# Splitting the first weight's conversion into two parts of four groups, in a fused attention and two-layer-pair kernel whose order is planned

## The chip, the cores and the metric

The kernel runs on one core of one Trainium2 chip. The metric is the device time of one execution in microseconds (us), lower is better. The kernel before took 978.41 us (median of 3 runs, 978.08 to 980.85).

## The reference

Masked attention over 4 batches, 8 heads, 576 positions and a head size of 64, in float32; its output (2304 tokens of 512) goes through two feed-forward blocks one after the other, each with weights of 512 x 2048 and 2048 x 512. The weights arrive as float64.

```python
scores = np.matmul(q, k.transpose(0, 1, 3, 2)) / np.sqrt(64)
thresh = np.max(scores, axis=-1, keepdims=True) - tau
scores = np.where(scores >= thresh, scores, -1000000000.0)
attn = np.exp(scores - np.max(scores, axis=-1, keepdims=True))
attn = attn / (np.sum(attn, axis=-1, keepdims=True) + 1e-09)
x = np.matmul(attn, v)                      # then (2304, 512)
h = x @ w_in                                # first block: moe_
sp = np.where(h > 20.0, h, np.log1p(np.exp(np.minimum(h, 20.0))))
x = (h * np.tanh(sp)) @ w_out
h = x @ w_in                                # second block: moe2_, other weights
return (h * np.clip(h + 3.0, 0.0, 6.0) / 6.0) @ w_out
```

## The kernel before

**Attention.** The 32 (batch, head) slices are worked on as 16 pairs of heads, four pairs a batch. An attention tile is 128 queries of one head against all 576 keys. TensorE writes its scores into one of two score buffers (line 1847), VectorE takes the negated peak (`nm_pk`, line 1856), ScalarE the threshold (1861) and the exponential (1866), VectorE masks (`e_ex`, line 1869), ScalarE writes the high float16 part of the result (1874), GpSimd its low part (a subtraction, line 730, `p_ph`), a transposing DMA on SP's queue turns both (`pt_tr`, 1882), and TensorE multiplies with V (1895). V too is split in a high part (ScalarE, line 1792) and a low part (VectorE, line 1797, `vl`). After two tiles of each head of a pair, VectorE normalises (1965 to 1972), TensorE transposes (`aux_fl`, 2009), and ScalarE and VectorE write the result's high and low float16 part into the block's input `x` (`x_fl`, lines 2018 and 730). A batch has 36 tiles: the first 16 complete block 2b (256 tokens), the other 20 block 2b + 1 and the tail of 64 positions. So block 0's input is ready some time after the 16th tile, block 1's after the 36th. A ninth block holds the four tails.

**The feed-forward layers.** Each weight has 8 groups. A group of the first two weights is 1 MB of float64 words, which arrive by one DMA (`raw_lr`, two buffers) and are turned into two float16 parts: VectorE takes the maximum (`top`, line 786), a small matmul spreads it over the partitions, VectorE makes the scales (798 to 803), ScalarE expands the high words (920), GpSimd multiplies (two instructions, line 927), VectorE joins the low words (line 940), ScalarE writes the high part (959), GpSimd the low part (two instructions, line 730, `w__h`). In this trace the groups of `w_in` have the buffer names `cvt_c__1_` 373, 443, 683, 826, 956, 1260, 1378 and 1599, their weight tiles `w__h__1_` 532, 616, 793, 972, 1172, 1375, 1510 and 1734, in this order.

The first layer (`inner` and `gemm1`, line 1239) works on a block group by group: 24 matmuls of 256 columns into one buffer `h`, taken by ScalarE or VectorE with a scale (1288, 1290) and stored to DRAM. Blocks 0 to 5 are worked on between attention's matmuls (`PIECE` = 2 matmuls at a time), blocks 6 to 8 after them. All its matmuls are one chain (`chain["g1"]`): they are issued in the order in which `inner` is called, block after block. The rest follows after attention: Mish and the first block's output matmul (`first_layer`, line 1354, `y_y`, with the second weight), then the second block (`second_layer`, lines 1428 and 1581).

**What sets the order.** When the program is built, a planner (`Plan`) replays all tasks with a cost for each engine and a due time, and appends them to the engines' queues in the order that it finds. On the chip each engine works its queue in order and waits by semaphores; the planned times themselves have no effect there. A task becomes a candidate when what it depends on is planned; each engine takes, of the candidates that can start first (within a small window), the one with the smallest due time. Due times are counted in steps: attention tile t is due at `START + t * STEP`, its product with V `PV_OFF` steps later, its block's input `PV_OFF + FLIP` steps later. Group g of the first weight is due at `START + CONV_AT * STEP + 2 * g * STEP`, hence at 27.1 us for the first and 66.2 for the last; the second weight's from `START + OUT_AT * STEP` = 430 us on. V's loads are due from `START - V_FIRST * STEP` on. Block 0's first-layer work is due from `START + (16 + MOE_LAG) * STEP` on, block 1's from 36 steps in place of 16. `NUDGE` moves the due times of single tasks by name; it has 1596 entries. `WHO` says which engines may take which task: K's scaling (`kh`) is ScalarE's (line 1767), V's low part VectorE's. Some tasks are `idle`: they issue no instruction and only take planned time on VectorE. `input_scales` writes the factors with which the first layer's results are taken, for batch 0 in four parts of two groups, for the other batches once all groups are there.

Of the kernel before, what the change touches and what calls it, by code (L numbers as in the profile page):

```python
# [10 lines left out]
F16 = mybir.dt.float16  # L11
# [36 lines left out]
STEP = 2.791  # L48
START = 12
PV_OFF = 3.422  # L50
V_FIRST = -0.435
FIRST_AHEAD = 3
PREP_AHEAD = 5.76
CONV_STEP = 1
CONV_AT = 5.423
LATE_STEP = 3.76
OUT_STEP = 2.681
OUT_AT = 149.789
V_AHEAD = 4.749
MOE_OFF = 9.75  # L60
MOE_LAG = 13.595
RATE = 0.9
NX = 3
FLIP = 3.348
ALPHA = {"act": 7.907, "pe": 3.022}
FITS = 0.015
# [3 lines left out]
BACKLOG = 99.0  # L70
# [16 lines left out]
SLOW = 0.413  # L87
SLOW_LATE = 0.226
HASTE = -5.307
WHO = {  # L90
    "c20": ("dve",), "c21": ("pool",), "c30": ("pool", "dve"), "c31": ("pool", "dve"),
    "q2": ("pool",), "q3": ("pool", "dve"), "u20": ("dve",), "u21": ("pool",),
    "u30": ("pool",), "u31": ("pool", "dve"), "uy0": ("pool", "dve"), "uy1": ("dve",),
    "kh": ("act",), "vh": ("act",), "vl": ("dve",), "q": ("dve",), "o0": ("dve",), "o1": ("dve",),
# [3 lines left out]
JOIN = 2.448  # L98
JOIN_FROM = 340.468
STAY = 0.954  # L100
# [333 lines left out]
PAD = {"zp": 0.834, "zpy": 0.374, "zps": 1.772}  # L434
NEAR_LATE = {"pe": 0, "dve": 0.087, "act": 0, "pool": 0.606, "sp": 0.21}
OFF_LATE = 6.941
OFF_FINAL = 29.238
LATE_AT = 11.587
OFF_SECOND = 40

# [1784 lines left out]
```

## Time and profile before

| | |
|---|---|
| time, median of 3 runs | 978.41 us (978.08 to 980.85) |
| profiled execution | 978.92 us |
| its span | 977.1 us, 25813 instructions |
| TensorE matmuls | 919.2 us busy (94%) |
| VectorE | 769.6 us (79%) |
| ScalarE | 650.0 us (67%) |
| GpSimd | 402.3 us (41%) |

The span runs from the first to the last thing that the profiler recorded; the time of the profiled execution is 1.8 us longer. In what follows PE is TensorE's matmuls and PEld its weight loads, DVE is VectorE, ACT ScalarE, POOL GpSimd, SP the engine that issues the DMAs (SPq its queue), and L940 is line 940 of the kernel. A busy share over the whole span is a mean over stages with different limits, so the rows further below are cut by stage. Instructions of one engine can overlap by a little; busy time counts an instant once. The granted clock (PEclk) is that of TensorE as a share of its upper level, 2.4 GHz; its other level is 1.2 GHz.

### The profile page before, as it was taken

How to read it: one execution, taken by the hardware profiler on the slowest of the kernel's cores; microseconds unless marked ns; L12 is line 12 of the kernel's file. 1: busy time of each engine (PE TensorE's matmuls, PEld its weight loads, DVE VectorE, ACT ScalarE, POOL GpSimd, SP SyncE). 2: the span in 40 equal slices, each digit the busy share in tenths (PEclk: the TensorE clock that was granted, in tenths of full speed). 3: DMA queues.
4: the chain of work that ended last, by engine and by line, in shares of the span. 5: the costliest groups of instructions: out<-in, count | busy, mean ns of one | idle time of the engine just before them, and what ended most of it. 6: DMA issues, size and time to landing. Idle time of an engine off the chain costs nothing.

```text
span 977.1 us, 25813 instructions
## 1 busy us (share of the span) xinstructions
PE 919.2 (94%) x10776; PEld 794.8 (81%) x10776; DVE 769.6 (79%) x1444; ACT 650.0 (67%) x1051; POOL 402.3 (41%) x354
## 2 busy tenths in 40 slices
PE   3669689999999999999999999999999999999996
PEld 1447457777777778888888888999999999999986
DVE  7988698888888887469999889787767767758864
ACT  6778688888888877568866778565354444444541
POOL 2777576756655767225656777710000000000000
PEclk9879799999999999999999999999999999999999
DMA  9899999999999999864665756760110110110001
GB/s 319 192 237 226 235 232 232 242 252 224 231 231 273 205 221 237 254 247 165 232 217 187 274 188 265 250 224 2 60 61 2 60 58 6 60 41 22 23 17 29
DMA packets 201796, 164.46 MB, mean 168 GB/s; under 512 B 174160, under 2 KB 174928, under 8 KB 195280
## 3 DMA queue, kind: packets, MB, share of 16 engines
q1 hardware_dynamic: 201680, 162.82, 61.6%
q8 instruction: 85, 1.39, 0.6%
q14 instruction: 31, 0.25, 0.1%
HBM read 84.28 MB, written 36.04 MB: 123 GB/s over the span
## 4 chain that ended last, share of the span: by engine, by line
PE 77%; DVE 11%; DMA 3%; POOL 3%; ACT 2%; issue 2%; SPq 1%; DVEq 0%; ACTq 0%; POOLq 0%
PE h_g L1239 15%; PE y_y L1354 13%; PE s_s L1847 8%; PE aux_pv L1895 6%; PE h_g0a L1428 5%; PE hp_g1a L1428 5%; PE hp_g1d L1428 2%; PE h_g0d L1428 2%; DMA raw_lr<-in_moe_w_in 2%; DVE top L786 1%; DVE e_ex L1869 1%; PE h_g1b L1428 1%; PE hp_g0b L1428 1%; POOL p_ph L730 1%; DVE gs_h L1334 1%
## 5 line engine op out<-in xcount | busy, mean ns | idle before, releaser
L730 POOL TENSOR_TENSOR p_ph<-e_ex,p_ph 128x128 f16<-128x128 f32 (+3 forms) x160 | 186.3, 1187 | 108.7 <-issue 54.8
L1581 PEld LDWEIGHTS <-gs_h 128*128 128x128 f16 x1512 | 146.6, 98 | 18.3 <-issue 1.5
L1428 PEld LDWEIGHTS <-w__h 128*128 128x128 f16 x2016 | 155.8, 98 | 0.6
L1856 DVE TENSOR_REDUCE nm_pk<-s_s 128x1 f32<-128x576 f32 x144 | 104.6, 750 | 29.6 <-PE s_s L1847 28.5
L1869 DVE SCALAR_TENSOR_TENSOR e_ex<-s_s,thr_th,e_ex 128x576 f32<-128x576 f32 x144 | 111.7, 810 | 18.4 <-ACT thr_th L1861 13.6
L1866 ACT ACTIVATE e_ex<-s_s,nm_pk 128x576 f32<-128x576 f32 x144 | 104.2, 730 | 17.9 <-DVE nm_pk L1856 14.0
L1847 PE MATMUL s_s<-kd_lk,qs_qp 64*128 64x288 f32 x440 | 81.3, 485 | 36.4 <-DVE e_ex L1869 27.6
L1874 ACT ACTIVATE p_ph<-e_ex 128x576 f16<-128x576 f32 x144 | 95.2, 679 | 13.0 <-DVE e_ex L1869 9.9
L1428 PEld LDWEIGHTS <-w__u 128*128 128x128 f16 x1008 | 98.5, 98 | 0.0
L1895 PEld LDWEIGHTS <-pt_tr 128*128 128x128 f16 x2016 | 79.9, 102 | 10.9 <-issue 6.1
L1847 PEld LDWEIGHTS s_s<-kd_lk,qs_qp 64*128 64x128 f32 x440 | 42.1, 207 | 57.3 <-issue 40.3
L730 DVE TENSOR_TENSOR gs_h<-g_ab,gs_h 128x896 f16<-128x896 f32 x72 | 74.5, 1085 | 15.9 <-ACT gs_h L1531 15.9
L1895 PE MATMUL aux_pv<-vh,pt_tr 128*128 128x65 f16 (+1 forms) x1296 | 84.7, 202 | 1.5 <-DMA pt_tr<-p_ph 1.3
L1531 ACT ACTIVATE gs_h<-g_ab 128x1792 f16<-128x1792 f32 x36 | 59.6, 1690 | 27.4 <-DVE g_ab L730 27.4
L1895 PE MATMUL aux_pv<-vl_vl,pt_tr 128*128 128x64 f16 x720 | 69.6, 201 | 0.0
L1515 ACT ACTIVATE g_ab<-g_ab,aux,hscales 128x512 f32<-128x512 f32 x72 | 54.1, 805 | 16.9 <-DVE g_ab L1456 16.9
L1288 ACT ACTIVATE he_t<-h_g,hin 128x512 f32<-128x512 f32 x63 | 42.9, 683 | 21.6 <-PE h_g L1239 17.7
L1325 ACT ACTIVATE hp_e<-hl_l 128x512 f32<-128x512 f32 x72 | 42.4, 595 | 21.5 <-DVE gs_h L1334 21.0
L1521 DVE SCALAR_TENSOR_TENSOR g_ab<-g_ab,f 128x512 f32<-128x512 f32 x72 | 51.1, 745 | 5.0 <-ACT g_ab L1515 5.0
L1334 DVE SCALAR_TENSOR_TENSOR gs_h<-hp_e,fscales,gs_h 128x512 f16<-128x512 f32 x72 | 52.9, 742 | 2.2 <-ACT gs_h L1328 1.9
L1328 ACT ACTIVATE gs_h<-hp_e,fscales 128x512 f16<-128x512 f32 x72 | 47.4, 679 | 9.7 <-PE y_y L1354 9.1
L1446 ACT ACTIVATE s_ka<-h_g0a 128x512 f32<-128x512 f32 x27 | 16.1, 595 | 48.4 <-PE h_g0a L1428 48.2
(653 smaller groups left out, 2522.7 us busy)
## 6 DMA issues: line engine op xcount, KB each, us to landing
hd<-he_t SPq DMA_DIRECT2D x36, 512.0 KB, 4.1
hl_l<-hd SPq DMA_DIRECT2D x18, 1024.0 KB, 5.9
raw_lr<-in_moe_w_in SPq DMA_DIRECT2D x16, 1024.0 KB, 5.8
raw_lr<-in_moe_w_out SPq DMA_DIRECT2D x16, 1024.0 KB, 7.4
yd<-yl_zhy SPq DMA_DIRECT2D x9, 896.0 KB, 3.8
qs_qp<-in_q SPq DMA_DIRECT2D x10, 576.0 KB, 5.7
v_lv<-in_v SPq DMA_DIRECT2D x16, 320.0 KB, 4.7
kd_lk<-in_k SPq DMA_DIRECT2D x15, 288.0 KB, 4.1
```

The source lines that it names most:

```text
L730: engine[e].tensor_tensor(dst, a, b, ALU.subtract)
L1239: mm(hv[:, j, :], wj[:, wl, c * P : (c + 1) * P], x.tile[:, c, xl, :], start=j == 0 and n == 0, stop=j == 1 and n == 11, skip_group_check= ...
L1334: nc.vector.scalar_tensor_tensor(s.tile[:, k, 1], g.tile.rearrange("p (a n) -> p a n", a=2), fs[:, fp : fp + 1], s.tile[:, k, 0], ALU.mult ...
L1354: mm(yv[:, h, :], wt[1][f // 2].tile[:, f % 2, wl, c * P : (c + 1) * P], gs[fp // COL].tile[:, fp % COL, gl, f % 2, :], start=fp == 0 and ...
L1428: mm(dst.tile[:, i * Q : (i + 1) * Q], wt[2][fp][wl].tile[:, right - 1, c * P : (c + 1) * P], x[xl].tile[:, c, left - 1], start=first and ...
L1581: mm(region(p), part[:, gl, left - 1], wt[3][fp][wl].tile[:, right - 1], start=fp == n == 0 and spot(p)[1] == 0, stop=fp == NG - 1 and n == 2,
L1847: mm(s[j].tile[:, half, :HALF], lh[r], rh[r], start=m == 0, stop=m == len(terms) - 1,)
L1856: nc.vector.tensor_reduce(neg.tile[:, j : j + 1], sv(j), AX.XY, ALU.max, negate=True)
L1866: nc.scalar.activation(ev(j), sv(j), AF.Exp, bias=neg.tile[:, j : j + 1])
L1869: nc.vector.scalar_tensor_tensor(ev(j), sv(j), thr.tile[:, j : j + 1], ev(j), ALU.is_ge, ALU.mult)
L1874: nc.scalar.activation(p16.tile[:, js, :S], e_.tile[:, js], AF.Copy)
L1895: mm(ov[:, dst, :d], pt.tile[:, j, ch, :], part.tile[:, src, vc, :], start=i == j == ch == 0 and part is vh, stop=j == w - 1 and ch == 8, ...
```

## The change

The first weight (`w_in` of the first block) is converted in two parts. Groups 0 to 3 (`FIRST` = 4) are due from `START + CONV_AT * STEP` on, which is now 7.0 us, and 5.6 us apart. Groups 4 to 7 are due from `START + SECOND_AT * STEP` = 120.6 us on and 8.4 us apart. The weight's summary is due at step 150. The first layer does block 0 with groups 0 to 3, then block 1 with groups 0 to 3, then block 0 with groups 4 to 7, then block 1 with these. Blocks 0 and 1 have two input buffers of their own (`r_xa`), and the three of `r_x` are left to the later ones. Batch 1's input scales are made in four parts like batch 0's, and for groups 4 to 7 of both batches become due when they are ready.

In the planner the `idle` tasks go, some assumed costs change, and the constants are new: START 12 to 9.178, STEP 2.791 to 2.786, PV_OFF 3.422 to 2.279, FLIP 3.348 to 3.912, V's first loads due at START + 0.841 steps in place of 0.435, BACKLOG 99 to 8 (a DMA other than a transpose is planned only when the planned backlog of DMAs is under 8 us), the second weight due from 455 us on and 8.9 us a group (430 and 15.0 before). K's scaling goes from ScalarE to GpSimd; V's low part stays on VectorE. `NUDGE` shrinks from 1596 entries to 121, of which 115 names were there before, most with other values. In the core of the diff, without `NUDGE` and some constants:

```diff
-PV_OFF = 3.422
-V_FIRST = -0.435
+PV_OFF = 2.279
+V_FIRST = -0.841
-CONV_AT = 5.423
+CONV_AT = -0.767
-BACKLOG = 99.0
+BACKLOG = 8
-    "kh": ("act",), "vh": ("act",), "vl": ("dve",), "q": ("dve",), "o0": ("dve",), "o1": ("dve",),
+    "kh": ("pool",), "vh": ("act",), "vl": ("dve",), "q": ("dve",), "o0": ("dve",), "o1": ("dve",),
+SUM_AT = 150
+FIRST = 4
+SECOND_AT = 40.0
+SECOND_STEP = 1.507
...
             at = prio + 2 * g * off
+            if m == 0 and g >= FIRST:
+                at = START + (SECOND_AT + 2 * (g - FIRST) * SECOND_STEP) * STEP
             task = tasker(at)
...
-        a = task({"dve": 1.28}, idle if m < 2 else c3, b, [raw, t], "c" + nm)
-        a = task({"dve": 1.28}, c4, [a], [raw, t], "c" + nm)
+        if m > 1:
+            b = [task({"dve": 1.28}, c3, b, [raw, t], "c" + nm)]
+        a = task({"dve": 1.28}, c4, b, [raw, t], "c" + nm)
...
-        parts = len(scaled_parts) if i == 0 else 1
+        parts = len(scaled_parts) if i < 2 else 1
...
+            if i < 2 and part * NG // parts >= FIRST:
+                task = tasker(None)
-            after = scaled_parts[part] if i == 0 else [f for fs in scaled_parts for f in fs]
+            after = scaled_parts[part] if i < 2 else [f for fs in scaled_parts for f in fs]
...
-    def inner(blk, early, at=None, gap=0.0):
+    def inner(blk, early, at=None, gap=0.0, fps=range(NG)):
...
-        for fp in range(NG):
+        for unit, fp in enumerate(fps):
...
+    r_xa = ring("xa", ap, 2, [P, NCH, 2, BLK], F16)
...
-                    x_of[blk] = Buf(r_x), []
+                    x_of[blk] = Buf(r_xa if blk < 2 else r_x), []
...
-                inner(blk, True, at, gap)
+                if blk == 0:
+                    inner(0, True, at, gap, range(FIRST))
+                elif blk == 1:
+                    gap *= NG / (2 * NG - FIRST)
+                    inner(1, True, at, gap, range(FIRST))
+                    inner(0, True, at + FIRST * gap, gap, range(FIRST, NG))
+                    inner(1, True, at + NG * gap, gap, range(FIRST, NG))
+                else:
+                    inner(blk, True, at, gap)
```

## Rows read from the trace of the kernel before

**Rows 1.** Busy time by stretch: length, engines' busy us, clock, DMA share, GB/s.

```profile
core 0: us, PE busy (x) PEld busy (x) DVE busy (x) ACT busy (x) POOL busy (x), PEclk, DMA share, GB/s
0.00:72.00 72.00, 39.98 (x368) 26.83 (x369) 60.70 (x116) 51.52 (x88) 43.28 (x52) 0.83 0.91 250
72.00:98.00 26.00, 24.84 (x283) 19.73 (x281) 21.30 (x47) 22.23 (x42) 20.12 (x20) 1.00 0.97 227
98.00:120.00 22.00, 14.18 (x132) 9.16 (x130) 13.54 (x32) 14.28 (x25) 11.67 (x14) 0.77 1.03 227
120.00:140.00 20.00, 15.80 (x178) 11.46 (x178) 17.75 (x40) 17.77 (x34) 16.13 (x14) 0.91 1.04 256
140.00:380.00 240.00, 238.04 (x2882) 185.69 (x2881) 200.24 (x363) 199.74 (x371) 151.46 (x141) 1.00 1.08 235
380.00:420.00 40.00, 39.84 (x456) 35.52 (x455) 23.29 (x55) 23.69 (x44) 14.71 (x14) 1.00 0.84 257
420.00:900.00 480.00, 478.48 (x5671) 443.47 (x5669) 380.80 (x696) 290.71 (x415) 144.92 (x102) 1.00 0.36 129
...
sum 977.00, PE 919.25 PEld 794.79 DVE 769.60 ACT 650.04 POOL 402.29; mean PE 114.91 PEld 99.35 DVE 96.20 ACT 81.25 POOL 50.29
```

**Rows 2.** The masks of attention (line 1869) by stretch: VectorE's busy time, count.

```profile
72.00:120.00 48.00, 10.26 (x13) 0.89 1.00 227
120.00:140.00 20.00, 4.87 (x7) 0.91 1.04 256
140.00:380.00 240.00, 76.50 (x99) 1.00 1.08 235
```

**Rows 3.** Groups, 0 to 140 us: count, busy us, mean ns, idle before.

```profile
L786 DVE TENSOR_REDUCE top<-raw_lr 128x1 f32<-128x1024 f32 x9 | 10.9, 1214 | 6.2 <-DMA raw_lr<-in_moe_w_in 6.1
...
L730 POOL TENSOR_TENSOR w__h__1_1172<-cvt_c__1_956,w__h__1_1172 128x512 f16<-128x512 f32 x2 | 2.3, 1158 | 4.3 <-ACT w__h__1_1172 L959 4.3
...
L765 DVE TENSOR_REDUCE top<-aux_zp 128x1 f32<-128x128 f32 x8 | 2.3, 281 | 0.1
...
L927 POOL TENSOR_TENSOR cvt_c__1_956<-cvt_c__1_956,eight 128x512 int32<-128x512 int32 x2 | 2.1, 1056 | 0.8 <-ACT cvt_c__1_956 L920 0.8
...
L801 DVE TENSOR_SCALAR sc<-sc 128x1 f32<-128x1 f32 x9 | 1.4, 153 | 0.3
...
L920 ACT ACTIVATE cvt_c__1_956<-raw_lr,sc 128x1024 f32<-128x1024 f32 x1 | 1.3, 1255 | 0.0
...
L940 DVE SCALAR_TENSOR_TENSOR cvt_c__1_956<-raw_lr,cvt_c__1_956 128x1024 uint32<-128x1024 uint32 x1 | 1.2, 1215 | 0.0
```

**Rows 4.** Waits of VectorE, 72 to 140 us: total, times, longest.

```profile
DVE nm_pk L1856 <- PE s_s L1847: 8.2, 9, 2.5
DVE top L786 <- DMA raw_lr<-in_moe_w_in: 3.6, 1, 3.6
```

**Rows 5.** The chain of waits near 110 us: start, length, what.

```profile
106.36 5.80 DMA raw_lr<-in_moe_w_in
```

**Rows 6.** First-layer matmuls from 60 to 220 us: count, durations, first and last start.

```profile
L1239 PE MATMUL h_g<-x_fl,w__h__1_532 x72: 271/273/273, 72.4 to 187.3; 128*128 128x256 f16 x72
```

**Rows 7.** First-layer matmuls (line 1239) by stretch: TensorE's busy time, count, weight loads.

```profile
72.00:140.00 68.00, 25.02 (x196) 18.28 (x196) 0.90 1.01 236
140.00:380.00 240.00, 125.57 (x1034) 95.78 (x1033) 1.00 1.08 235
```

**Rows 8.** Conversions (line 940) by stretch: VectorE's busy time, count.

```profile
140.00:260.00 120.00, 4.86 (x4) 1.00 1.06 232
260.00:380.00 120.00, 2.43 (x2) 1.00 1.11 238
```

**Rows 9.** Timeline: a mask, the last part of block 1's input; start, length.

```profile
118.72 0.81 DVE L1869 SCALAR_TENSOR_TENSOR e_ex<-s_s,thr_th,e_ex 128x576 f32<-128x576 f32 x1
...
133.82 0.38 ACT L2018 ACTIVATE x_fl<-aux_fl 128x256 f16<-128x256 f32 x1
```

**Rows 10.** Timeline at 72 us: GpSimd's subtractions and a conversion on VectorE.

```profile
72.39 2.51 POOL L730 TENSOR_TENSOR p_ph<-e_ex,p_ph 128x128 f16<-128x128 f32 x2 [0.58 <-ACT p_ph L1874]
...
73.97 2.01 DVE L940 SCALAR_TENSOR_TENSOR cvt_c__1_826<-raw_lr,cvt_c__1_826 128x1024 uint32<-128x1024 uint32 x1
```

More of the change, by code (lines that the diff above doesn't have):

```diff
@@ L46 @@
 RELEASE = dict.fromkeys(("s", "m", "h", "y", "aux"), 0.27)
-STEP = 2.791
-START = 12
-PV_OFF = 3.422
-V_FIRST = -0.435
+STEP = 2.786
+START = 9.178
+PV_OFF = 2.279
+V_FIRST = -0.841
 FIRST_AHEAD = 3
-PREP_AHEAD = 5.76
+PREP_AHEAD = 5.025
 CONV_STEP = 1
-CONV_AT = 5.423
[L56 to L59, printed above, removed]
+CONV_AT = -0.767
+LATE_STEP = 1.5
+OUT_STEP = 1.601
+OUT_AT = 160
+V_AHEAD = 4.836
 MOE_OFF = 9.75
-MOE_LAG = 13.595
-RATE = 0.9
+MOE_LAG = 13.701
+RATE = 0.918
 NX = 3
-FLIP = 3.348
-ALPHA = {"act": 7.907, "pe": 3.022}
-FITS = 0.015
+FLIP = 3.912
+ALPHA = {"act": 6.878, "pe": 2.26}
+FITS = 0
 PORT = ("vl", "c", "u", "o", "zs", "q", "p")
@@ L86 @@
 SLACK = 0
-SLOW = 0.413
-SLOW_LATE = 0.226
-HASTE = -5.307
+SLOW = 0.187
+SLOW_LATE = 0.293
+HASTE = -3.433
 WHO = {
-    "c20": ("dve",), "c21": ("pool",), "c30": ("pool", "dve"), "c31": ("pool", "dve"),
-    "q2": ("pool",), "q3": ("pool", "dve"), "u20": ("dve",), "u21": ("pool",),
-    "u30": ("pool",), "u31": ("pool", "dve"), "uy0": ("pool", "dve"), "uy1": ("dve",),
-    "kh": ("act",), "vh": ("act",), "vl": ("dve",), "q": ("dve",), "o0": ("dve",), "o1": ("dve",),
+    "c20": ("pool", "dve"), "c21": ("dve",), "c30": ("pool",), "c31": ("pool", "dve"),
+    "q2": ("pool", "dve"), "q3": ("pool",), "u20": ("dve",), "u21": ("pool", "dve"),
+    "u30": ("pool", "dve"), "u31": ("pool",), "uy0": ("pool", "dve"), "uy1": ("dve",),
+    "kh": ("pool",), "vh": ("act",), "vl": ("dve",), "q": ("dve",), "o0": ("dve",), "o1": ("dve",),
 }
@@ L97 @@
 PARTS = 4
-JOIN = 2.448
-JOIN_FROM = 340.468
-STAY = 0.954
+SUM_AT = 150
+FIRST = 4
+SECOND_AT = 40.0
+SECOND_STEP = 1.507
+JOIN = 3.144
+JOIN_FROM = 409.647
+STAY = 0.782
 NBLK_EARLY = 2 * B - 2
@@ L103 @@
 NUDGE = {
[323 rows of a table removed]
[25 rows of a table added]
 }
-EASE = {"mk": -6, "ph": 2.117, "pl": 0.391, "tr": 1.5, "ex": 2.281, "s": -5.48, "th": -2.308}
+EASE = {"mk": -6, "ph": 0.526, "pl": -1.615, "tr": 1.702, "ex": 1.842, "s": -6, "th": -1.651}
 P_LO = ("pool",)
@@ L432 @@
 LATE = {"gs": 2, "hl": 2, "h": 2, "y": 2}
-WINDOW = {"pe": 0.17, "dve": 0.095, "act": 0.232, "pool": 0.789, "sp": 0}
[L434 to L438, printed above, removed]
+WINDOW = {"pe": 0.186, "dve": 0.095, "act": 0.226, "pool": 0.722, "sp": 0}
+PAD = {"zp": 0.827, "zpy": 0.3, "zps": 2.577}
+NEAR_LATE = {"pe": 0.013, "dve": 0.075, "act": 0, "pool": 0.694, "sp": 0.21}
+OFF_LATE = 7.635
+OFF_FINAL = 29.067
+LATE_AT = 9.931
 OFF_SECOND = 40
@@ L806, in group_scale @@
         if m % 2 == 0:
-            a = task({"dve": 0.15}, idle, [a], [], "za" + name)
             a = spread(task, name, lambda: top, [], ring, a)
-        return task({"dve": 0.97 if m == 0 else 0.5}, factor, [a], [], "zf" + name)
+        return task({"dve": 0.8 if m == 0 else 0.38}, factor, [a], [], "zf" + name)
     def summary(task, m, ring, after):
@@ L902, in convert @@
             scaled_parts[:] = [factors[i : i + step] for i in range(0, NG, step)]
-        scaled_by[m] = summary(tasker(prio + 2 * NG * off), m, ring, factors)
-    def idle(e):
-        pass
+        at = START + SUM_AT * STEP if m == 0 else prio + 2 * NG * off
+        scaled_by[m] = summary(tasker(at), m, ring, factors)
     def one_conversion(m, g, raw, deps, task):
@@ L1231, in link, with gemm1 @@
         return chain[name]
-    def gemm1(task, m, fp, piece, x, h, ready):
+    def gemm1(task, m, fp, piece, x, h, ready, unit):
         def mms(j, first, end):
@@ L1249, in gemm1 @@
             last = link(
-                task, "g1", fp, piece, lambda a, b, j=j: mms(j, a, b),
+                task, "g1", unit, piece, lambda a, b, j=j: mms(j, a, b),
                 ready + [converted[m, 2 * fp + j]], [x, h, wt[m][fp]], f"g{fp}{j}_",
@@ L1275, in inner @@
         else:
-            x, ready = x_of.pop(blk)
+            x, ready = x_of[blk]
         hscale, scaled = hin[:, blk // 2], hin_done[blk // 2]
-        for fp in range(NG):
+        for unit, fp in enumerate(fps):
             h = Buf(r_h)
-            last = gemm1(task, 0, fp, PIECE if early else 12, x, h, ready)
+            last = gemm1(task, 0, fp, PIECE if early else 12, x, h, ready, unit)
             if fp % 2 == 0:
@@ L1290, in take @@
                     nc.vector.tensor_scalar(dst, h.tile, f, None, ALU.mult)
-            taken.append(task(TAKE, take, [last, scaled[fp]], [h, he], f"t{fp}", 0.0, fp + VECTOR))
+            taken.append(task(TAKE, take, [last, scaled[fp]], [h, he], f"t{fp}", 0.0, unit + VECTOR))
             if fp % 2:
@@ L1298, in inner @@
                 h_stored[blk, fp // 2] = task(
-                    {"sp": 0.5}, put, taken, [he], f"s{fp}", HD_DMA, fp + VECTOR
+                    {"sp": 0.5}, put, taken, [he], f"s{fp}", HD_DMA, unit + VECTOR
                 )
@@ L1934, in query_tiles @@
                 size = (js.stop - js.start) * S
-                cost = {"dve": 0.17 + size / 960.0, "pool": 0.1 + size / 450.0}
+                cost = {"dve": 0.17 + size / 960.0, "pool": 0.35 + size / 490.0}
                 parts.append(
```

348 rows, old and new, of the table NUDGE are left out of this document.

## The prediction

> **What bounds the kernel now.** I read the whole span first and then its stages, because a share over the whole span hides where time can be won. TensorE is busy for 919 of 977 us [rows 1], so the time is TensorE's work, plus what it idles, plus what it loses at a lowered clock. The stages show where that is: 32.0 us idle up to 72 us, 13.2 from 72 to 140, 2.0 from 140 to 380, 0.2 to 420, 1.5 to 900 [rows 1]. The granted clock is below its upper level in the first 140 us and full from there to 900. So from 140 to 900 us TensorE has no room. A gain can only be made before, by work done earlier, and all of it then reaches the end, as TensorE behind is full.
>
> What holds TensorE back before 140 us is read from VectorE. Every attention tile (128 queries of a head) needs a peak and a mask there. From 72 to 120 us come 13 masks, 3.7 us a tile; from 140 to 380 us 99, 2.42 us a tile [rows 2]. In the slow stretch VectorE also converts the first weight: its eight group maxima, and the first of the second weight, all stand before 140 us [rows 3]. From 72 to 140 us VectorE waits 8.2 us for scores and 3.6 for a raw weight load [rows 4]; the chain of waits shows that load, 5.8 us, as what ended last at 112 us [rows 5]: the maximum waits for it at the head of VectorE's queue, and the masks stand behind.
>
> The other half of the picture is the filler, the first layer's matmuls between attention's. Block 0's begin at 72.4 us [rows 6], and by 140 us all eight groups of 24 and four more are done [rows 7].
>
> **The change, part by part.**
>
> *Groups 4 to 7 move behind.* One group costs VectorE 1.214 + 0.281 + 1.215 and four small ops of 0.15, 3.3 us [rows 3], so four cost 13.2; GpSimd 2 x 1.056 + 2 x 1.158 = 4.4, so 17.7; ScalarE an expansion of 1.255 and a copy of as many elements, some 2.5, so 10; and SP's queue four loads of 1 MB, which no longer stand among the transposes. Nothing is saved, all of it is done later: the new due times begin at 9.178 + 40 x 2.786 = 120.6 us and are 8.4 us apart. There these groups take the place of the second weight's, six of which are converted between 140 and 380 us [rows 8], far ahead of their due times (430 us and later). Those move on into VectorE's room: 39.8 us are free from 140 to 380, 16.7 from 380 to 420 [rows 1]. That hides them; with that cover gone they would cost their 13.2 us.
>
> *Block 0 stops after four groups* until block 1's first four are done, as these matmuls are chained in order. So from 72 us until block 1's input is there TensorE has only 4 x 24 x 125.57/1034 = 11.6 us of filler [rows 7]. Block 1's input came 14.7 us behind the mask that ended at 119.5 us, at 134.2 [rows 9].
>
> *What the attention does with the room.* Without conversions a tile cost VectorE (200.24 - 6 x 3.3)/99 = 1.82 us from 140 to 380 [rows 1, 2, 8], so VectorE alone would allow some 2 us. The rate seen with TensorE full is 2.42. I take a rate between 2.2 and 2.42 from 72 us on. A tile's share of TensorE was (238.04 - 125.57)/99 = 1.14 us [rows 1, 2, 7]. At 2.42 us: 13 masks after 72 us are done at 103.5, block 1's input is there at 118.2; until then 46.2/2.42 = 19.1 tiles x 1.14 + 11.6 = 33.4 us of work; then TensorE is full, 21.8; 55.2 by 140 us. At 2.2, by the same steps, 34.1 + 24.7 = 58.8. Before, the busy 54.8 us less 14.18 x 0.23 + 15.80 x 0.09 = 4.7 for the clock are 50.1 [rows 1]; by unit costs, 20 tiles x 1.14 + 196 x 0.121, they are 46.6 [rows 2, 7]. Between these, 48.4, the gain is 6.8 and 10.4; with all bounds 5.1 to 12.2. I take the middle, 8.6.
>
> *Earlier hand-over.* PV_OFF + FLIP fall from 6.77 steps (18.9 us) to 6.19 (17.2), so a block's input is due 1.6 us sooner. Bounds 0 and 1.6; I take 0.8, since due times only order work.
>
> *The first 72 us.* The first four groups are due from 7.0 us on, ahead of most tiles, not from 27.1. VectorE does the same tiles and groups in it, in another order. Bounds: a gain of one maximum with its small ops, some 2 us, and the loss of one raw load that stands ahead of V's, 5.8 [rows 5]; I take 0.
>
> *K's scaling moves to GpSimd* and leaves ScalarE. No row has it on GpSimd; the nearest are 1.06 and 1.16 us for 128x512 [rows 3], so some 1.2 to 1.3 for 128x576, 16 times in 400 us; GpSimd is busy 151 of the 240 us from 140 to 380 [rows 1]. It can also stop VectorE: an op with two inputs in SBUF that met GpSimd's subtractions took 2.01 us and ended 1.1 us behind them; another took 1.215 [rows 3, 10]. Bounds: 0, and 16 x 0.8 = 13 us of VectorE if each met such an op. These ops (16 of V's low part, 16 conversions) are about a tenth of VectorE's time, so I take 1.3 us of VectorE's room and nothing of TensorE's.
>
> The Trainium skill, SBUF — State Buffer, "SBUF: two separate sides", speaks against this move: VectorE and GpSimd share a port pair as an exclusive lock, and whoever comes second is blocked for the other's whole instruction. By it a meeting costs up to all of GpSimd's 1.3 us, 2 us of VectorE's room in place of 1.3; the 2.01 us agree with it.
>
> *Small parts.* The stand-in tasks that leave the planner issued no instruction. Batch 1's input scales become four ScalarE instructions in place of one, under 1 us, in ScalarE's room [rows 1]. Blocks 0 and 1 get x buffers of their own, so holding block 0 longer blocks no other block.
>
> *A new plan everywhere.* The nudges fall from 1596 to 121 and most due times change. From 140 to 900 us TensorE idles only 3.6 us [rows 1], so this can hardly win there: bounds 0 and three times as much again, 11; I take 2.0, half as much again.
>
> Against the profiled execution of 978.92 us (span 977.1 and 1.8 around it; the runs' median is 0.5 less) the sum is - 8.6 - 0.8 + 2.0 = - 7.4, so **971.5**.
>
> **The rivals.**
>
> *Slower: block 0 runs out of filler.* If attention doesn't speed up, because its rate is set by the loop from scores over peak, exponential and mask back to the score buffers, TensorE has less to do than before. At 3.2 us a tile block 1's input is there at 128.3: 17.6 x 1.14 + 11.6 + 11.7 = 43.4 against 48.4, a loss of 5.0, and with the plan's 2.0 the time is 985.9. It decides at 2.87 us a tile. For it: 3.7 us now, and VectorE waits longer for scores than for loads [rows 2, 4]. Against it: 2.42 us later, with the same score buffers.
>
> *No change: the second half comes late.* From 140 to 260 us the conversions of lowest rank came one in 30 us [rows 8]. The filler is 125.57/240 = 52% of TensorE there [rows 7]; a group now opens two units, 5.8 us, which last 11 us. At 15 us a group TensorE lacks 4 x (15 x 0.52 - 5.8) = 8 us, the whole gain: 979. For it: VectorE is at 83% there [rows 1]. Against it: due times 8.4 us apart, ahead of all tiles behind step 49.
>
> *The new plan loses its density:* with 11 us in place of 2.0 the time is 980.5.
>
> *More than forecast:* if the first 72 us tighten too (32 us idle), or a tile takes 2.0 us, 958 to 966.
>
> **How the numbers follow.** About 0.3%, 2.9 us, is what a measurement of this kernel can tell from no change (its runs lie 2.8 us apart). The forecast, 966 to 975.5: 0.43. More than that: 0.14. A small gain or none, by a late second half or a looser plan: 0.25, of which 0.09 still end below 975.5. Slower, by the filler, 981.3 to 990: 0.18. So faster 0.66, same 0.16, slower 0.18. The range 960 to 983 leaves out about a third of the "more" case and most of the slower one, near 0.2.
>
> **What would show it.** Right: no maxima of groups 4 to 7 before 100 us; some 19 masks from 72 to 118 us; block 1's first matmul before 122 us; TensorE idle under 8 us from 72 to 140 us, its clock at the upper level from 100 us on. Wrong: 13 to 15 masks there; a hole of over 12 us on TensorE ahead of block 1's input; first-layer matmuls that wait for conversions behind 140 us; more than 6 us idle from 140 to 900 us; a first y matmul that waits for the second weight.

## The result, and the profile after

The changed kernel takes 989.18 us (median of 4 runs, 986.93 to 990.63), the kernel before 979.41 beside it (978.08 to 980.85): a ratio of 1.0091 [1.0071, 1.011]. It is slower by 9 us where the forecast was a gain of 7, and outside the range. The profiled span is 988.4 us, 11.3 longer than before.

TensorE first, by the stretches of [rows 1]: length, each engine's busy time, granted clock, DMA share, GB/s.

```profile
0.00:72.00 72.00, 37.74 (x328) 24.75 (x328) 59.34 (x115) 46.93 (x78) 53.79 (x57) 0.98 0.89 233
72.00:98.00 26.00, 20.92 (x242) 15.39 (x240) 16.70 (x30) 15.93 (x33) 13.99 (x14) 0.93 1.01 219
98.00:120.00 22.00, 16.85 (x190) 12.47 (x190) 19.84 (x44) 19.37 (x39) 16.84 (x17) 0.89 1.05 213
120.00:140.00 20.00, 15.98 (x177) 11.59 (x178) 16.02 (x31) 14.31 (x27) 14.77 (x12) 0.86 0.95 221
140.00:380.00 240.00, 232.00 (x2780) 182.51 (x2778) 202.65 (x372) 189.15 (x347) 169.32 (x151) 0.99 1.09 232
380.00:420.00 40.00, 39.34 (x474) 33.61 (x471) 24.73 (x61) 23.45 (x45) 21.49 (x21) 1.00 0.93 215
420.00:900.00 480.00, 479.56 (x5621) 444.13 (x5620) 381.22 (x695) 293.51 (x422) 137.75 (x100) 1.00 0.39 140
```

TensorE's idle time is 34.3 us up to 72 us (32.0 before), 14.2 from 72 to 140 (13.2), 8.0 from 140 to 380 (2.0), 0.7 to 420 (0.2), 0.4 to 900 (1.5). With the end that is 66.6 us against 57.9; the other 2.6 us of the span are busy time, although the mean granted clock rose from 0.979 to 0.988. The room that the forecast wanted to fill, 72 to 140 us, is as empty as it was, and a new hole stands behind it. From 420 us on TensorE idles no more than before.

The masks of attention and the first layer's matmuls by stretch, as in [rows 2] and [rows 7]:

```profile
72.00:120.00 48.00, 12.61 (x17) 0.91 1.03 216
120.00:140.00 20.00, 5.20 (x7) 0.86 0.95 221
140.00:380.00 240.00, 72.64 (x94) 0.99 1.09 232
...
72.00:140.00 68.00, 17.13 (x138) 0.90 1.00 218
140.00:380.00 240.00, 126.21 (x1041) 0.99 1.09 232
```

Attention did run faster from 72 to 120 us, 17 masks in place of 13. It was paid for in filler: 138 first-layer matmuls in place of 196. The end of the n-th mask, counted in VectorE's timelines, shows where the tiles are won and lost (us):

```
mask            16     24     36     50     60     70    100    144
before        50.2   76.7  119.5  156.4  181.2  208.4  278.7  389.1
after         57.2   83.2  115.8  152.9  187.1  214.4  287.0  398.5
```

Seven us are lost by the 16th mask, the last that block 0 needs. Ten are won between the 24th and the 36th, where the kernel before converts its second half. Nine are lost again between the 50th and the 60th, and 3.5 more to the end.

The filler in TensorE's timeline: start, length, tile, count. The first row is the last piece of block 0's fourth group, the second the first piece of block 1.

```profile
103.51 1.05 PE L947 MATMUL h_g<-xa_fl,w__h__1_743 128*128 128x256 f16 x8
128.63 0.61 PE L947 MATMUL h_g<-xa_fl,w__h__1_335 128*128 128x256 f16 x4
```

Between them lie 24 us without a first-layer matmul. The same stretch in the changed kernel and then in the kernel before (columns as above):

```profile
104.60:128.60 24.00, 15.97 (x176) 10.92 (x174) 19.93 (x41) 18.67 (x36) 17.96 (x17) 0.79 1.07 245
```
```profile
104.60:128.60 24.00, 17.77 (x185) 12.58 (x183) 15.97 (x34) 17.48 (x34) 16.76 (x17) 0.86 0.98 233
```

What TensorE waits for from 72 to 140 us, then from 140 to 420 us (total, times, longest):

```profile
PE aux_pv L1604 <- DMA pt_tr<-p_ph: 5.9, 3, 3.5
PE s_s L1556 <- DVE e_ex L1578: 5.4, 5, 2.9
...
PE aux_pv L1604 <- DMA pt_tr<-p_ph: 8.0, 9, 3.0
PE s_s L1556 <- DVE e_ex L1578: 0.3, 1, 0.3
```

The same rows of the kernel before, not shown ahead of the prediction:

```profile
PE s_s L1847 <- DVE e_ex L1869: 7.7, 2, 4.5
PE s_s L1847 <- issue: 2.9, 1, 2.9
PE aux_pv L1895 <- DMA pt_tr<-p_ph: 0.9, 2, 0.7
...
PE aux_pv L1895 <- DMA pt_tr<-p_ph: 0.4, 1, 0.4
```

So 13.9 us of waiting for the transposing DMAs ahead of the products with V stand against 1.3. The chain of waits of the changed kernel from 72 to 140 us is held by them too, where that of before named a raw load [rows 5]:

```profile
72.42 10.83 DMA pt_tr<-p_ph
...
87.50 8.68 DMA pt_tr<-p_ph
...
114.77 6.28 DMA pt_tr<-p_ph
```

Two of the second half's maxima are not late at all. VectorE's timeline (the bracket is the idle time before the row):

```profile
71.20 1.21 DVE L492 TENSOR_REDUCE top<-raw_lr 128x1 f32<-128x1024 f32 x1
...
81.33 1.22 DVE L492 TENSOR_REDUCE top<-raw_lr 128x1 f32<-128x1024 f32 x1 [3.51 <-DMA raw_lr<-in_moe_w_in]
```

A due time sorts candidates and holds nothing back, so an engine with nothing more urgent takes them. VectorE waits 3.5 us at its queue's head for a raw load, as it did before [rows 4].

### The profile page after: what moved, and what is told of

Same layout as the page of the kernel before. It is cut to its first block, busy times and chain, and to the rows that moved or that the text cites. A ratio compares the mean times of both kernels' runs of the same rounds, so it can differ in the third digit from the quotient of the medians.

```text
span 988.4 us, 25840 instructions
## 1 busy us (share of the span) xinstructions
PE 921.8 (93%) x10776; PEld 798.3 (81%) x10776; DVE 779.5 (79%) x1453; ACT 639.4 (65%) x1030; POOL 428.0 (43%) x369
## 4 chain that ended last, share of the span: by engine, by line
PE 69%; DMA 11%; DVE 8%; POOL 6%; issue 2%; ACT 2%; SPq 1%; DVEq 0%; POOLq 0%; ACTq 0%
PE h_g L947 13%; PE y_y L1062 12%; DMA pt_tr<-p_ph 9%; PE s_s L1556 5%; PE hp_g1a L1136 5%; PE h_g0a L1136 5%; PE aux_pv L1604 4%; POOL p_ph L436 3%; PE hp_g1d L1136 2%; PE h_g0d L1136 2%; PE h_g1b L1136 1%; PE hp_g0b L1136 1%; DVE gs_h L1042 1%; PE y_y__1_8_0_15017 L1289 1%; PE y_y___1_5_0_13258 L1289 1%
## 5 line engine op out<-in xcount | busy, mean ns | idle before, releaser
L1556 PE MATMUL s_s<-kd_lk,qs_qp 64*128 64x288 f32 x440 | 81.8, 489 | 26.6 <-DVE e_ex L1578 13.9
L1604 PE MATMUL aux_pv<-vh,pt_tr 128*128 128x65 f16 (+1 forms) x1296 | 85.9, 202 | 14.2 <-DMA pt_tr<-p_ph 13.9
L996 ACT ACTIVATE he_t<-h_g,hin 128x512 f32<-128x512 f32 x59 | 40.3, 684 | 21.5 <-PE h_g L947 18.4
L1036 ACT ACTIVATE gs_h<-hp_e,fscales 128x512 f16<-128x512 f32 x72 | 47.1, 679 | 1.4 <-PE h_zp L468 0.9
```

The source lines that it names most:

```text
L1556: mm(s[j].tile[:, half, :HALF], lh[r], rh[r], start=m == 0, stop=m == len(terms) - 1,)
L1604: mm(ov[:, dst, :d], pt.tile[:, j, ch, :], part.tile[:, src, vc, :], start=i == j == ch == 0 and part is vh, stop=j == w - 1 and ch == 8, ...
```

## The experiments

The letters in the expectations: F, the split itself costs, as block 0's later matmuls leave a stage that had room for them; P, the order that the new plan gives; K, K's scaling on GpSimd; the others say what they are. The new kernel is "after". A ratio is to the kernel before, run beside it; a difference in us is the difference of two ratios times 980.

**One part undone, planned anew.**

```diff
-FIRST = 4
+FIRST = 8
```

> The changed kernel with FIRST = 8: the first weight is converted in one part, with due times 5.6 us apart from 7 us on, and block 0 is done with all eight groups before block 1; all other constants and nudges are the changed kernel's. If the split costs the time (block 0 leaves TensorE without filler, theory F), this gains back most of the 10 us: 979 to 982, with over 180 first-layer matmuls done by 140 us in place of 138. If the new constants and the short list of nudges cost it (theory P), it stays at 986 to 992, and TensorE still waits for transposes some 8 us from 140 to 400 us.

1000.3 us, 1.0209 [1.0164, 1.0255]. The whole weight in one part with all the other new constants is slower than after, by 11.6 us. That doesn't clear the split, as the constants were chosen with it.

The other way round, the kernel before with the split's code; a few assumed costs are after's, the other constants and all nudges are before's. The edit against before begins so:

```diff
+SUM_AT = 150
+FIRST = 4
+SECOND_AT = 40.0
+SECOND_STEP = 1.507
...
```

> The changed kernel's code, split in two parts of four groups, but with all planner constants and all 1596 nudges of the kernel before (K's scaling on ScalarE, PV_OFF 3.422, BACKLOG 99). Theory F (the split itself starves TensorE): 984 to 990, with some 140 first-layer matmuls by 140 us. Theory P (new constants): 972 to 979, as the split is then left with its gain. The old nudges were fitted to another set of tasks, so 2 to 4 us of either may be theirs.

1019.42 us, 1.0402 [1.0376, 1.0428], with 28 us of TensorE idle between 420 and 900 us, where neither kernel idles 2; 17.5 of them are one wait of the second block for the load of its input. The 144th mask, the last, ends at 398.4 us, as late as in after (398.5; 389.1 in before). So with the constants of before the attention loses as much, by the split or by nudges that were fitted to another set of tasks; this run doesn't tell which.

```diff
-PV_OFF = 2.279
-FLIP = 3.912
+PV_OFF = 3.422
+FLIP = 3.348
```

> The changed kernel with PV_OFF 3.422 and FLIP 3.348 of the kernel before, planned anew: the products with V stand 3.2 us further behind their scores in TensorE's queue. If TensorE stands at products whose transposes are still under way because they were planned too early (part of theory P), the 13.9 us that it waits for transposes before 400 us fall below 5 and the time to 980 to 985. By theory F alone it stays within 2 us of the changed kernel.

1008.11 us, 1.0277 [1.0252, 1.0302]; TensorE's wait for transposes up to 420 us rose from 13.9 to 20.0 us. All three miss both theories. In e1 and e2 a new plan and the edit can't be told apart; in e4 the edit alone may do it, as later products in an order that stays cost as much (e17, below). From here on instructions were changed in an order that stays, but for e11 and e12, which have no nudges at all, and for the products with V that e9, e10, e17 and e18 move on TensorE's queue.

**The order kept, one part changed.**

```diff
-                nc.gpsimd.tensor_scalar(kv, kv, qscale, None, ALU.mult)
+                nc.scalar.activation(kv, kv, AF.Copy, scale=qscale)
```

> The changed kernel's plan as it is, but K's scaling is issued on ScalarE instead of GpSimd at the same place of the order (0.7 us each in place of 1.73). If GpSimd at 20 of 20 us from 20 to 40 us delays the tiles, the transposes and block 0's input (77.0 us in place of 72.4; theory K), 3 to 6 us come back: 983 to 986. If not, within 1.5 us of the changed kernel.

988.72 us, 1.0088 [1.006, 1.0115], as after. K falls as a cause, though GpSimd's price was mis-sized: these ops take 1.73 us each (last section).

Next the conversions of groups 4 to 7 were left out but for their small scale ops (loads, maxima, expansion, joins, both parts), and their matmuls read the weights of groups 0 to 3; first in the order of before, then in that of after.

```diff
+LEFT_OUT = ("lr0_4", "lr0_5", "lr0_6", "lr0_7")
...
-            wj = wt[m][fp].tile[:, j]
+            wj = wt[m][fp % 4].tile[:, j]
```

> The kernel before in its own order, with the conversion of groups 4 to 7 left out except its small scale ops (four loads of 1 MB, four maxima, expansions, shifts, joins and both parts; some 9.7 us of VectorE, 9.1 of ScalarE, 17.7 of GpSimd); the matmuls of these groups use the weights of groups 0 to 3. It is the most that moving them away can give while block 0 keeps its filler. By the prediction's step (VectorE's room lets attention run faster) the time falls by 6 to 12 us, to 967 to 974. By theory F alone (the room is worth little, TensorE's order and its filler set the rate) it falls by 0 to 3.

974.81 us, 0.9952 [0.9934, 0.9969]. Taking these conversions away altogether, loads too, is worth 4.7 us in before. The forecast had given 8.6 us for moving them.

> The changed kernel in its own order, with the same left out. If the second part, now between 116 and 167 us, takes VectorE from attention where TensorE needs every tile (21 masks from 140 to 200 us in place of 25; theory D), the time falls by 4 to 8 us, to 981 to 985. If it is hidden there, as predicted, by less than 2.

982.37 us, 1.0029 [1.0005, 1.0053], so 6.1 us less than after. The later place isn't hidden; the conversions cost there about what they cost in front (the intervals overlap). Without them the 50th to the 60th mask still take 32.1 us (24.8 in before), so these conversions are not what slows that stretch. TensorE from 72 to 140 us in e6:

```profile
72.00:140.00 68.00, 57.85 (x675) 43.49 (x672) 51.57 (x104) 48.67 (x97) 40.25 (x38) 0.92 0.99 191
```

The filler by itself: 22 of the 24 matmuls in each of block 0's groups 4 to 7 were left out, 88 in all.

```diff
             for n in range(first, end):
+                if short and n != 11 * j:
+                    continue
```

> The kernel before in its own order, with 22 of the 24 matmuls left out in each of groups 4 to 7 of block 0 (88 matmuls, 9.6 us of TensorE). Theory F says that they stood between 90 and 139 us where TensorE would else idle: the time falls by 0 to 4 us. If the stage were full they would be worth 9.6.

982.34 us, 1.0034 [1.0015, 1.0054]: no gain but a small loss, with a clock of 0.76 from 72 to 140 us (0.90 in before). In before these matmuls stand in time that TensorE would idle or work through at a lower clock.

> The changed kernel in its own order, with the same 88 matmuls left out, which now stand between 151 and 180 us. Theory F: TensorE is full there, the time falls by 7 to 10 us, to 979 to 982, and the difference to the same cut in the kernel before is what moving them costs. If TensorE waits there for VectorE or for transposes anyway (theories D and P), it falls by less than 4.

987.73 us, 1.0084 [1.0046, 1.0122], as after within the interval. In after they stand at 151 to 174 us, and there too nothing clear of noise is gained without them (0.7 us, within about 4): from 150 to 180 us TensorE's busy time falls from 28.2 to 22.9 us and its clock from 1.00 to 0.83, and the masks come no sooner (34.4 us from the 50th to the 60th, 34.2 in after). What sets that stretch isn't TensorE's work. That doesn't exclude F: the stage that they left lost 3.3 us without them (e7).

**The wait at the products with V.** In e9 and e10 each product was issued behind up to 12 pieces of filler that directly follow it, in e17 and e18 behind up to 3.2 us of any work, scores too.

```diff
-            task.fn(e)
+            self.emit(task, e)   # keeps a "pv" task until what may pass it has been issued
```

> The order of after, with one change on TensorE's queue: a product with V is issued behind the pieces of first-layer work (up to 12, of two matmuls each) that directly follow it, instead of ahead of them. Nothing is left out and nothing is planned anew. Theory P (TensorE loses its time standing in order at products with V whose transposes are under way, 14 us before 400 us against 1.3 in before): the work that can go stands ahead, this wait falls to 4 to 8 us and the time to 980 to 985 us. Rival R (the pace of the attention sets the time, and the stand is only where the slack becomes visible): the idle time moves to another wait, and the time stays within 1.5 us of after, 987.5 to 990.5.

989.88 us, 1.0102 [1.0083, 1.012]. P in this form misses; up to 420 us the wait for transposes falls from 13.9 to 10.7 us only. From 140 to 420 us:

```profile
PE aux_pv L1629 <- DMA pt_tr<-p_ph: 6.1, 5, 2.8
PE s_s L1581 <- DVE e_ex L1603: 1.6, 3, 1.2
PE aux_fl L1743 <- DVE xn_dn L1706: 1.2, 2, 1.0
PE h_g L972 <- POOL w__h__1_2251 L461: 1.1, 1, 1.1
```

What the products no longer wait, the scores, the block's input and a late weight part do.

> The same change on the order of before, which waits only 1.3 us at products with V before 400 us. Theory P: nothing to win, within 1.5 us of before, 978.5 to 981.5. Rival R: the same, or 1 to 3 us slower where a later product holds back a buffer of the attention. If it is faster by over 2 us, the stand is not what tells the two kernels apart.

982.57 us, 1.0036 [1.0018, 1.0055]; rival R's side, a little beyond it.

**Without nudges.** `NUDGE = {}` in each, planned anew.

> After with all its 121 nudges of single due times taken out, and planned anew. Theory P (what the split could win is lost to a plan that is fitted less closely): 992 to 1005 us, and below the kernel before without its nudges by 5 us or more. Rival F (working on half a weight at a time costs by itself): not below the kernel before without its nudges.

998.5 us, 1.0192 [1.0169, 1.0215].

> Before with all its 1596 nudges taken out, and planned anew. Theory P: these nudges are worth far more than the 121 of after, 1000 to 1030 us. Rival F: 985 to 1000 us, at or below after without its nudges.

994.43 us, 1.015 [1.013, 1.0169]. P misses again and F holds here: without a nudge after is still the slower by 4 us, though the intervals touch. The 1596 nudges are worth 15 us to before, the 121 10 us to after. So about half of the 9 us, with an error nearly as large, is there before any nudge, and the rest could be the looser fit. The short list is in the main no new fit: of the 115 names that both lists have, 80 have the same value in both, where "The change" says that most differ.

**The transposing DMAs.** They turn only the high parts and the tails, 10 of 18 blocks; the products read a high part's block where the low part's would stand.

```diff
-                    out=pt.tile[:, :w].rearrange("p a c n -> p (a c) n"),
-                    in_=p16.tile[:, :w].rearrange("p a n -> p (a n)"),
+                    out=pt.tile.rearrange("p a c n -> p (a c) n")[:, : 5 * w],
+                    in_=p16.tile.rearrange("p a n -> p (a n)")[:, : (S + TAIL) * w],
```

> The order of after; the transposing DMAs turn only the high parts and the tails (10 of 18 blocks), and the products with V read a high part's block where the low part's would stand, so the low parts but the tails' are left out of the result. All engines have the same instructions. Theory D (what after loses before 400 us it loses to transposing DMAs that land late): TensorE's wait for them falls from 14 us to under 4 and the time by 6 to 12 us, to 977 to 983. Rival R (the pace is set by the circle of the engines' own queues, and the DMA is only where it shows): at most 3 us less, 986 to 989.

973.32 us, 0.9933 [0.9913, 0.9953], 15.5 us less than after; the wait for transposes up to 420 us falls from 13.9 to 1.5 us. The cut takes out more than packets, though. GpSimd makes a low part by two instructions, the tail's of 0.4 us first; the larger one, of 2.1 us, now writes where the DMA doesn't read, and the DMA no longer waits for it. GpSimd and SP's queue in after, then in e13:

```profile
216.40 2.52 POOL L436 TENSOR_TENSOR p_ph<-e_ex,p_ph 128x128 f16<-128x128 f32 x2 [2.30 <-issue]
218.95 4.00 SPq L1591 DMA_TRANSPOSE pt_tr<-p_ph  x1
```
```profile
205.25 2.52 POOL L436 TENSOR_TENSOR p_ph<-e_ex,p_ph 128x128 f16<-128x128 f32 x2 [2.30 <-issue]
205.71 1.47 SPq L1599 DMA_TRANSPOSE pt_tr<-p_ph  x1
```

> The same cut in the order of before, whose TensorE waits 1.3 us for these DMAs before 400 us. Theory D: at most 3 us less, 976.5 to 980. Rival R: as much less as in after, within 1.5 us. If before falls by 6 us or more too, the DMAs hold both kernels and do not tell them apart.

970.58 us, 0.9894 [0.9876, 0.9912], 10.4 us less than before. Both are more than theory D said. From 72 to 420 us a transposed block lands on average 3.3 us (e13) and 3.2 us (e14) sooner behind its tile's last mask; 1.4 and 1.3 us of that is a shorter time from issue to landing, the rest, the larger part, an earlier issue. So the transposes together with their wait for GpSimd hold both kernels, after more; what the DMA alone is worth these runs don't tell. Of the 0.91% between the kernels 0.39% is left, so somewhat over half goes with this cut (0.52%, within about 0.33). TensorE from 72 to 140 and from 140 to 380 us in e13, then in e14:

```profile
72.00:140.00 68.00, 58.69 (x672) 44.09 (x673) 57.60 (x111) 53.63 (x103) 50.83 (x46) 0.92 0.90 187
140.00:380.00 240.00, 238.20 (x2864) 189.38 (x2862) 208.35 (x383) 195.39 (x362) 174.46 (x157) 1.00 0.79 188
```
```profile
72.00:140.00 68.00, 59.95 (x647) 44.38 (x643) 57.84 (x123) 57.57 (x105) 50.76 (x49) 0.90 0.84 219
140.00:380.00 240.00, 239.07 (x2921) 188.16 (x2921) 199.88 (x360) 201.42 (x375) 154.89 (x143) 1.00 0.74 180
```

From 72 to 140 us both gain about as much (4.9 and 5.1 us of busy time). They differ behind: the hole of after from 140 to 380 us is gone (1.8 us idle in place of 8.0), where before had little to win (2.0).

**VectorE's room in the first 72 us.** Groups 0 to 3 lose their joins of the low words and three of the four maxima.

```diff
         def c4(e):
+            if m == 0 and g < 4:
+                return
```

> The order of after without VectorE's four joins of the low words in groups 0 to 3 and without three of their four maxima (group 0's stands for them): 4 x 1.21 + 3 x 1.21 = 8.5 us less on VectorE in the first 72 us, all else issued. Theory V (the four conversions beside V's low parts on VectorE make block 0's input late): its first matmul from 77.0 us to 71 to 73, and 4 to 6 us less, 983 to 985. Rival G (GpSimd's queue and the transposes behind it set that time): first matmul not before 75.5 us, the time within 2 us of after.

986.34 us, 1.0055 [1.0038, 1.0073]. V holds for the place: block 0's first matmul starts at 71.41 us in place of 76.96. For the price it doesn't: 5.5 us earlier there is 3.5 us less at the end.

> The same cut in the order of before, where these four groups stand spread up to 72 us. Theory V: 0 to 3 us less than before, 976.5 to 980. Rival G: the same. If it gains as much as after does, VectorE's room in the first 72 us is worth the same in both and does not tell them apart.

977.72 us, 0.9976 [0.9963, 0.999], 2.4 us less. Nearly the same, so it hardly tells the kernels apart.

**Products held back further**, as above.

> The order of after, with each product with V held back on TensorE's queue behind work of any kind, scores too, up to 3.2 us of planned TensorE time (the 1.143 steps by which PV_OFF fell), unless the next product, a task that needs it or its buffers' next use comes first. Nothing is left out. Theory D1 (the DMAs land as they did in before, and only the products were put too early in TensorE's order): TensorE's wait for transposes falls from 14 us to under 5 and the time to 980 to 984 us. Rival D2 (the transposes themselves are late, by full DMA engines and a late start, and hold the attention's buffers and the blocks' inputs whatever the order on TensorE): the time stays within 2 us of after, 987 to 991, with the wait moved to the scores or to the first layer.

1018.05 us, 1.038 [1.035, 1.041].

> The same change in the order of before, whose products stood 3.2 us later already and wait 1.3 us for transposes before 400 us. D1: 0 to 4 us slower than before, 979 to 984, as the normalising and the blocks' inputs come later. D2: the same. If it is faster by over 2 us, products were too early in both orders.

1014.15 us, 1.0344 [1.0306, 1.0381]. The wait for transposes is gone from e17, and from 72 to 420 us these have its place:

```profile
PE s_s L1589 <- DVE e_ex L1611: 17.6, 26, 2.1
PE aux_fl L1751 <- DVE xn_dn L1714: 9.4, 11, 1.6
```

D1 and D2 both miss: the edit costs 28 us in after and 34 in before. A product that goes later holds back the normalising and, by its order, more than it frees. So nothing shows that the products were put too early in TensorE's queue, but an edit that costs as much in before is no clean test of it. No version that does the whole work is faster than before.

## Why the prediction was wrong

**What bounds it.** That TensorE is the time, and that what it lacks before 140 us reaches the end, held: after 420 us the two kernels do the same. Of the 11.3 us of span 8.7 are idle time of TensorE, most of it behind 140 us, and 2.6 busy time. That VectorE is what holds TensorE back before 140 us was only part of it: without four conversions and their loads before gains 4.7 us (e5), with less to transpose, and that sooner, 10.4 (e14). The DMA column of [rows 1] stood beside it at 0.97 to 1.04 from 72 to 140 us and at 1.08 to 380, and wasn't read. The kernel before from 140 to 380 us and then from 420 to 900 us, by DMA packets:

```profile
DMA packets 124509, 56.43 MB, mean 235 GB/s; under 512 B 117051, under 2 KB 117051, under 8 KB 123707
...
q1 hardware_dynamic: 124475, 55.96, 107.6%
```
```profile
DMA packets 13117, 62.07 MB, mean 129 GB/s; under 512 B 1457, under 2 KB 1457, under 8 KB 9265
...
q1 hardware_dynamic: 13062, 61.26, 35.8%
```

With attention's transposes 235 GB/s go with a share of 1.08; without them 129 GB/s take 36%, so by an estimate a full share without them would carry some 360 (129/0.358). While attention runs 94% of the packets are under 512 B. The share is packet time, and as it goes above 1 it doesn't say how much more the engines could carry. Two readings of the prediction were off by little: the clock was at 1.00 from 72 to 98 us [rows 1], and 4 x 24 x 125.57/1034 is 11.7.

**The step that failed** is "What the attention does with the room". It gave VectorE's free time to the attention, 2.2 to 2.42 us a tile from 72 us on, and 8.6 us of gain. By its own count 72 to 140 us should have held 55.2 to 58.8 us of TensorE's work at the upper clock, against 50.1 before. After has 53.8 us busy there, which is 48.2 by the same step for the clock (20.92 x 0.07 + 16.85 x 0.11 + 15.98 x 0.14 = 5.6), and 1 us more of idle time than before. 17 masks in 48 us are 2.8 us a tile, at the point from which, by the text's own working, the change gains nothing (2.87). The 2.42 came from behind 140 us; that the loop of scores, peak, mask, low part, transpose and product would run at it ahead of 140 us was assumed. e6 is the direct test, with the filler where the change puts it: without any of the four conversions the 24th to the 36th mask come 2.6 us apart ((110.2 - 78.8)/12; 2.7 in after), and TensorE still idles 10.2 us from 72 to 140 us (14.2 in after), 4.8 of it at transposes and 3.2 at masks. In before the same cut gains 4.7 us, not 8.6 (e5).

**The rival "block 0 runs out of filler"** described the rest, in part: block 0's filler ended at 104.6 us and block 1's input was there at 128.1, not at 118.2; 24 us without filler, at a clock of 0.79. What moving the filler costs by itself isn't settled: e7 has 3.3 us lost where it left and e8 0.7 taken where it came, some 4 if they add, with an error as large.

**"That hides them"** was wrong. The due times at 120.6 us didn't keep the maxima of two groups from VectorE at 71 and 81 us, and the four groups together cost 6.1 us (e6), about half of the 13.2 that the text named for the cover gone. The hand-over from the 36th mask to block 1's input took 12.3 us (115.8 to 128.1, the end of VectorE's low part). The 14.7 of the prediction end with ScalarE's high part [rows 9]; VectorE's low part came at 135.2 us, 15.7 behind the mask. This step was on the safe side by 3 us, and the tiles ahead of it were late.

**"The first 72 us", taken as 0,** was a loss: by 72 us 21 masks have begun (23 in before), and block 0's first matmul moved from 72.4 to 76.96 us. The chain there goes over VectorE (a join and three of V's low parts, 40.1 to 44.6 us, then a maximum at 47.1, ahead of the masks of the tiles due) and then over GpSimd, whose low part of attention ended behind the conversions' at 64.8 us. e15 shows the first as the cause of the late input; by e15 against e16 it explains about 1 us of the difference between the kernels, within some 3.

**"A new plan everywhere", 2.0 us,** was mis-sized: from 140 to 900 us TensorE idles 9.1 us against 3.6 [rows 1], 5.5 more in place of 2.0, and 8.0 of the 9.1 are waits for transposes. The upper bound, 11, held. The rival "the second half comes late" didn't come: from 140 to 420 us no first-layer matmul of after waits for a weight. K's scaling was mis-sized by 40% and cost nothing that shows (e3).

**A rule weighed.** In the trace one of V's low parts takes 1.68 us beside a GpSimd subtraction and 0.87 alone; the slow one ends 0.68 us behind the subtraction (115.10 and 114.42 us). GpSimd's row, then VectorE's two:

```profile
111.91 2.51 POOL L436 TENSOR_TENSOR p_ph<-e_ex,p_ph 128x128 f16<-128x128 f32 x2 [0.16 <-issue]
```
```profile
98.16 0.87 DVE L1506 SCALAR_TENSOR_TENSOR vl_vl<-v_lv,vs_ve,vh 128x640 f16<-128x640 f32 x1
...
113.42 1.68 DVE L1506 SCALAR_TENSOR_TENSOR vl_vl<-v_lv,vs_ve,vh 128x640 f16<-128x640 f32 x1
```

The rule that the prediction named, the Trainium skill, SBUF — State Buffer, "SBUF: two separate sides" (the second to come waits for the other's instruction), agrees with these rows but for 0.2 us: after a wait for the whole subtraction the slow one would end 0.87 us behind it. Seven of the 32 low parts of V in the two traces take over 0.9 us, and each ends 0.68 us behind a GpSimd instruction that had begun before it.

**What stays open.** Why the transposes cost after more than before. From 72 to 420 us a transposed block lands on average 11.5 us behind its tile's last mask in after and 10.9 in before; the median from issue to landing, from 72 to 200 us, is 6.3 us in place of 5.3. The product starts 13.8 and 13.6 us behind the mask, so the 3.2 us by which PV_OFF fell in the plan aren't seen on the chip; but 16 of 72 products start within 0.2 us of the landing, 6 of 71 in before. Two changes of the order on TensorE won nothing (e9, e17), nor did K's scaling on ScalarE (e3). The loads of groups 4 to 7 are a small part: without them TensorE still waits 11.0 of the 13.9 us (e6). Left are the order on SP's queue, where K and Q loads are issued right ahead of the transposes at 72.4 and 87.5 us, the time at which GpSimd hands over the low parts, and the split's own part. Loads moved behind the transposes weren't tried.

## What to carry to other kernels

Before giving an engine's free time to a loop, ask what else the loop waits for in that stage, and read every shared resource there, the DMA column among them; a share near 1 with many small packets is a possible bound, to be tested like a busy engine. Leaving the work out altogether (e5, e6) prices a move in one run, and cheaply. A cut that lightens a transfer can also free it from a wait (e13), so look at when it starts as well as how long it takes. In a planned kernel a due time is no barrier, and a part tried with a plan made anew can move the time by more than the part: change instructions in an order that stays.

## What the hardware showed

K's scaling on GpSimd, one input from SBUF in float32 and a scale, written in float32, costs more per element than the two-input subtraction, which writes float16. GpSimd's groups up to 420 us (busy us, mean ns):

```profile
L436 POOL TENSOR_TENSOR p_ph<-e_ex,p_ph 128x1024 f16<-128x1024 f32 x64 | 137.0, 2140 | 0.0
...
L1478 POOL TENSOR_SCALAR kd_lk<-kd_lk,qscale 128x576 f32<-128x576 f32 x15 | 25.9, 1726 | 3.8 <-DMA kd_lk<-in_k 3.7
```

That is 3.0 ns for each element of a partition against 2.1. The forecast had scaled the two-input rows and expected 1.2 to 1.3 us.

Transposing 10 of 18 blocks, with an earlier start of the transposes, took 15.5 us from one kernel and 10.4 from the other, the largest gains of all the runs, in a kernel whose TensorE is busy 94% of the time.
